# Hashed attention and a layer-norm feed-forward on one core: the row scale behind the second product, another start, loads and preparations at other places

## The chip, the cores and the metric

The kernel runs on one core of one Trainium2 chip. A core has five engines that run their own instruction streams in order: TensorE (PE in the profile, with its weight loads as PEld), VectorE (DVE), ScalarE (ACT), GpSimd (POOL) and SyncE (SP). They meet through semaphores. Data moves between the main memory and the on-chip memory through 16 DMA engines; SP, ACT and POOL issue the transfers. Products of PE land in PSUM, a small memory that DVE and ACT empty.

The metric is the device time of one execution in microseconds (us). Besides it there is one profiled execution, with a record of every instruction; its span is the time from the first instruction to the last.

## The reference: what is computed

Attention with 4 batches, 8 heads, 768 rows and 64 columns per head. Each row of q and of k gets a bucket number of six bits, and only rows of the same bucket attend to each other. The result, with its 8 heads side by side (512 columns), goes through a layer norm and a feed-forward with 2048 hidden units and a residual.

```python
q_bits = (np.einsum('bhsd,dk->bhsk', q, proj) > 0)      # proj: 64 x 6
mask = q_bucket[:, :, :, None] == k_bucket[:, :, None, :]
scores = np.where(mask, scale * q @ k^T, -1e9)
attn = softmax(scores) @ v                              # 4 x 8 x 768 x 64
x = attn, heads side by side                            # 4 x 768 x 512
xn = (x - mu) / np.sqrt(var + 1e-06) * g_ln
out = x + np.maximum(xn @ w_ch1, 0.0) @ w_ch2
```

## The kernel before

**Units, steps, batches.** A unit is four heads of one batch, so there are 8 units (n = 0 to 7), two per batch. A unit has 24 steps (4 heads x 6 row tiles), a batch has 48, and the whole main loop has 192. In step i, `scores` (L413) multiplies 128 rows of k with all 768 rows of q (two products of 384 columns, L420) and ACT takes the exponential (L426); `attend` (L429) works two steps behind, with six products per step (L437). After the last tile of a head DVE divides and writes 64 columns of x (L449, L454, L455).

**The mask inside the product.** The six hash bits of each row are written beside its 64 values as plus or minus one half (for q times 800), so that a product over 70 rows gives the score and the mask together. Preparing one unit's k, and likewise its q, takes: a cast to bf16 into one of three `pads` on POOL (L137 or L148), a 32x32 block transpose of the values on DVE (`hash_turn`, tile hashT, one buffer), the product with proj on PE (`hash_mm_wide` L159 for units 0 and 1, `hash_mm` L189 for the others), a transpose of the result on DVE into `bits` (L163 or L196) and the bits into the pad (L167, L172 or L199, L203), and a transpose of the pad into `opT`: on PE for units 0 and 1 (`turn_wide`, L212, emptied by DVE L219 and ACT L217), by a DMA transpose from SP for units 2 to 7 (`turn`, L224). For v, POOL casts and adds (L230 to L235), and PE sums over all rows (`value_sum`, L241).

**What sets the order.** Each engine's order is the order of the code. `at(i, fn, ...)` puts a piece of work into step i, and `plan_unit(n)` (L246) spreads the preparation of unit n over the 24 steps of unit n-1 and puts the loads of unit n+1 between them. All loads but the first q go through SP's queue, and a load that waits for a free buffer holds what stands behind it. Buffers that matter: `hashnat` (2), `scorenat` (3), `hashT` (1), `opT` (4), and two PSUM buffers "mm" that the hash products, the PE transposes, the value sums and both feed-forward products share.

**Weights.** The 8.4 MB of weights arrive in 16 pieces (L291), which borrow the space of `hbuf` and `x`, and DVE casts them to bf16 (L298 with the factor g_ln, L302).

**Layer norm and feed-forward.** Statistics of x are gathered along the way (`stat`, L311). After the last step of a batch `rstd` (L313) finishes the means and variances (L317, L319) and finds 1/sigma with four Newton rounds of four small DVE instructions (L332 to L338). `normalize` (L348) then writes (x - mean)/sigma in two halves, `turn_x` (L357) transposes each by DMA, and `feed_forward` (L369) runs seven steps after the batch's last step: 64 products of the first kind per half (L378), emptied by DVE (L387) and ACT (L385) in turn, then 48 of the second (L393), whose sums DVE adds to x (L399) before the store. The feed-forward of batch b is a generator of which some 4.7 products are issued per step of batch b+1; that of the last batch runs after the main loop.

## Time and profile before

| | us |
|---|---|
| three runs | 391.26, 392.71, 386.02 (median 391.26) |
| the profiled execution | 386.11, of it span 384.2 |
| first scores of unit 0 | 30.88 after the start |
| first scores of unit 2 (step 48) | 88.72 |
| first feed-forward product | 104.73 |
| last x of the last batch done, first product of its feed-forward | 323.27, 335.60 |

Over the span PE is busy 84 %, DVE 54 %, ACT 52 %, POOL 19 %. The shares hide stages with different limits, so the profile is read by stages: the start up to the first scores, the first batch, the three stretches around a layer norm inside the main loop, and the end. In a table of stages "PEclk" is the share of its full clock that PE was granted, and the DMA share is the mean busy share of the 16 DMA engines.

### The profile page before, as it was taken

Reading aid. Unit: us, or ns where it says so; the run is one execution under the profiler, and the core shown is the slowest. Engines: PE = TensorE matmul, PEld = TensorE weight load, DVE = VectorE, ACT = ScalarE, POOL = GpSimd, SP = SyncE. Lnnn points to the kernel's source line nnn. Section 1 sums busy time; section 2 is a strip of 40 time slices with the busy share of each in tenths; the row PEclk is TensorE's granted clock in tenths of the full one; section 3 lists DMA queues with packets and bytes.
Section 4 is the critical chain, followed back from the end, with each engine's and each line's share of the span. In section 5 each row is a group of like instructions: output and inputs, shape, how many; then the busy total and the mean of one; then the engine's idle time right before and its main releaser. Section 6 shows DMA issues by size and latency. Waiting matters only on the chain.

```text
span 384.2 us, 6912 instructions
## 1 busy us (share of the span) xinstructions
PE 323.8 (84%) x2741; PEld 187.5 (49%) x2760; DVE 205.6 (54%) x496; ACT 198.5 (52%) x261; POOL 72.1 (19%) x76
## 2 busy tenths in 40 slices
PE   0678988827289999995999999959999999599995
PEld 0344655514146555652565556525655665254542
DVE  0343779975944555568444555794433555642321
ACT  1015589944348656762587568625876783031220
POOL 8366011615011420420105012400000000000000
PEclk9966999975769999998999999998999999899999
DMA  8559999994399598703994999028401000510102
GB/s 165 159 165 373 285 287 355 203 234 132 83 224 220 145 243 239 167 27 84 253 252 127 211 235 214 22 43 184 83 2 51 33 2 3 122 42 30 55 0 82
DMA packets 77168, 56.03 MB, mean 146 GB/s; under 512 B 52560, under 2 KB 70992, under 8 KB 77136
## 3 DMA queue, kind: packets, MB, share of 16 engines
q1 hardware_dynamic: 76304, 54.80, 57.9%
q10 hardware_dynamic: 576, 0.79, 1.0%
q8 instruction: 21, 0.34, 0.4%
q14 instruction: 11, 0.09, 0.1%
q0 software_dynamic: 256, 0.01, 0.1%
HBM read 36.71 MB, written 6.29 MB: 112 GB/s over the span
## 4 chain that ended last, share of the span: by engine, by line
PE 58%; DVE 20%; DMA 15%; issue 2%; ACT 2%; SPq 1%; POOL 1%; DVEq 0%; ACTq 0%
PE sc L420 11%; PE av L437 6%; DMA hashnat<-in_k_dram 5%; DVE x L455 3%; DMA scorenat<-in_v_dram 3%; DMA hashnat<-in_q_dram 3%; DVE xn L348 2%; DVE nd L449 2%; DMA wst<-in_moe_w_ch_dram 2%; DMA opT<-pad_98 2%; DVE x L399 2%; PE hp L189 2%; ACT expb L426 2%; PE hpw L159 1%; PE o_4214 L393 1%
## 5 line engine op out<-in xcount | busy, mean ns | idle before, releaser
L426 ACT ACTIVATE expb<-sc,bias_sb 128x768 bf16<-128x768 f32 x192 | 168.4, 905 | 97.2 <-PE sc L420 95.7
L420 PE MATMUL sc<-opT 70*128 70x384 bf16 x384 | 97.9, 338 | 15.1 <-DMA opT<-pad_98 8.6
L437 PEld LDWEIGHTS <-expb 128*128 128x128 bf16 x1152 | 62.5, 99 | 28.0 <-issue 3.7
L378 PEld LDWEIGHTS <-w_sb 128*128 128x128 bf16 x512 | 45.1, 98 | 36.9 <-issue 15.4
L420 PEld LDWEIGHTS <-opT 70*128 70x128 bf16 x384 | 37.3, 100 | 49.0 <-issue 26.4
L393 PEld LDWEIGHTS <-hbuf 128*128 128x128 bf16 x384 | 34.6, 99 | 49.4 <-issue 19.3
L449 DVE TENSOR_TENSOR nd<-av,vd 128x390 f32<-128x390 f32 x32 | 17.9, 559 | 32.7 <-PE av L437 32.6
L178 DVE STREAM_TRANSPOSE hashT<-hashnat 128x768 f32<-128x768 f32 x32 | 29.2, 950 | 9.0 <-DMA hashnat<-in_k_dram 9.0
L159 PE MATMUL hpw<-hashT,projB 128*128 128x384 f32 x32 | 17.3, 706 | 11.6 <-DVE hashT L178 11.6
L437 PE MATMUL av<-vaug_103,expb 128*128 128x65 bf16 x432 | 25.5, 196 | 0.0
L437 PE MATMUL av<-vaug_102,expb 128*128 128x65 bf16 x432 | 25.5, 196 | 0.0
L455 DVE TENSOR_TENSOR x<-nd,rec 128x384 f32<-128x384 f32 x32 | 20.5, 641 | 1.1
L437 PE MATMUL av<-vaug_104,expb 128*128 128x65 bf16 x288 | 17.2, 197 | 0.0
L311 DVE BATCH_NORM_STATS2 stats<-x 128x6 f32<-128x256 f32 (+1 forms) x48 | 17.0, 381 | 0.3
L159 PEld LDWEIGHTS hpw<-hashT,projB 128*128 128x128 f32 x32 | 8.5, 278 | 17.6 <-DVE hashT L178 11.4
L217 ACT COPY opT<-tp 70x768 bf16<-70x768 bf16 x4 | 3.2, 795 | 23.7 <-PE tp L212 23.7
L233 POOL TENSOR_TENSOR scorenat<-scorenat 128x768 f32<-128x768 f32 x8 | 15.1, 1890 | 0.2
L137 POOL CAST pad_98<-scorenat 128x1536 bf16<-128x1536 f32 x4 | 5.9, 1467 | 46.1 <-DMA scorenat<-in_k_dram 25.1
L137 POOL CAST pad_96<-scorenat 128x1536 bf16<-128x1536 f32 x4 | 5.9, 1467 | 45.5 <-DMA scorenat<-in_k_dram 24.9
L137 POOL CAST pad_97<-scorenat 128x1536 bf16<-128x1536 f32 x4 | 5.9, 1467 | 40.7 <-DMA scorenat<-in_k_dram 21.0
L189 PE MATMUL hp<-hashT,projT 128*32 128x192 f32 x192 | 11.6, 365 | 1.4 <-DVE hbuf L387 1.4
L163 DVE STREAM_TRANSPOSE bitsw<-hpw 128x384 f32<-128x384 f32 x8 | 4.7, 583 | 14.6 <-PE hpw L159 14.6
(368 smaller groups left out, 430.1 us busy)
## 6 DMA issues: line engine op xcount, KB each, us to landing
wst<-in_moe_w_ch_dram SPq DMA_DIRECT2D x16, 512.0 KB, 9.5
hashnat<-in_k_dram SPq DMA_DIRECT2D x32, 192.0 KB, 4.4
scorenat<-in_v_dram SPq DMA_DIRECT2D x8, 768.0 KB, 5.1
out_dram<-x SPq DMA_DIRECT2D x24, 256.0 KB, 2.1
hashnat<-in_q_dram SPq DMA_DIRECT2D x28, 192.0 KB, 4.7
scorenat<-in_k_dram SPq DMA_DIRECT2D x6, 768.0 KB, 7.1
scorenat<-in_q_dram SPq DMA_DIRECT2D x6, 768.0 KB, 6.9
hashnat<-in_q_dram ACTq DMA_DIRECT2D x4, 192.0 KB, 6.2
```

The source lines that it names most:

```text
L137: nc.gpsimd.tensor_copy(pad_of(n, key)[:, :, 0:D], sn.rearrange("p h (s d) -> p (h s) d", d=D))
L159: nc.tensor.matmul(hp[:, 0 : w * 32], projB[:, j, :], hT[:, 2 * f : 2 * f + 2, :, j, :], start=(j == 0), stop=(j == 1),)
L178: nc.vector.transpose(hT[:, 2 * i : 2 * i + 2].rearrange("p c s j t -> p (c s j t)"), hn[:, 2 * i : 2 * i + 2].rearrange("p c n -> p (c n)"),)
L189: nc.tensor.matmul(hp[c * 32 : (c + 1) * 32, 0 : NS * 32], projT[:, j, :], hT[:, c, :, j, :], start=(j == 0), stop=(j == 1),)
L311: nc.vector.bn_stats(norm[b][:, s, part, :], xs[b][:, s, c0:c1])
L378: nc.tensor.matmul(hp[:, 0:QH], w1_sb[:, o, n * P : (n + 1) * P], xT[:, :, o, :], start=(o == 0), stop=(o == ND - 1),)
L393: nc.tensor.matmul(o2, hb[:, n, i * P : (i + 1) * P], w2_sb[:, n, :], start=(n == 0), stop=(n == NH - 1),)
L420: nc.tensor.matmul(sc[:, f, 0:QH], kT[0:KB, h * NS + t, :], qT[0:KB, h * NS + f * HALF : h * NS + (f + 1) * HALF, :],)
L426: nc.scalar.activation(e, sc[:, :, 0:QH], AF.Exp, scale=scale, bias=bias_sb)
L437: nc.tensor.matmul(av[:, s * VA : (s + 1) * VA], e[:, s // HALF, (s % HALF) * P : (s % HALF + 1) * P], va[:, h, t, :], start=(t == 0 and s ...
L449: nc.vector.tensor_add(nd, av[:, 0 : NS * VA].rearrange("p (s n) -> p s n", n=VA), vd[:, h : h + 1, :].to_broadcast([P, NS, VA]),)
L455: nc.vector.tensor_mul(xs[b][:, :, hd * D : (hd + 1) * D], nd[:, :, 0:D], rec.to_broadcast([P, NS, D]),)
```

## The change

What it does, part by part:

- **Row scale.** `normalize` only subtracts the mean. 1/sigma multiplies the sum of the second product instead (one `scalar_tensor_tensor` in place of the add, L394 of the changed kernel); since 1/sigma is positive it passes through the maximum with zero. `rstd` is split: `mean` stays ahead of `normalize`, and three Newton rounds (12 instructions and a factor, on POOL) follow four steps later.
- **Start.** proj is loaded once into `proj4` (4 small transfers in place of 8) and copied into projT and projB by 8 small DVE copies. 64 products of a constant tile (`WARM`) stand first on PE. The pieces of k and of q of unit 0 are spread over SP's and ACT's queues, k first on both. The casts and block transposes of k and q come before both hash products. The zeroing of the pads covers only the columns behind the bits and comes after the value work of unit 0.
- **Loads.** Unit 1's hash rows go into `scorenat` buffers and its v into a `hashnat` buffer; they and weight pieces 0 to 11 stand ahead of unit 2's loads in SP's queue, at the start of the program. Unit 2's loads stand at steps 3, 13 and 14, weight pieces 12 to 15 behind them. The casts of the weights stand 2 to 10 steps earlier.
- **Preparation.** Within a unit's plan, k is at +0, +2, +3 (cast and block transpose, hash product, transpose to opT), q at +4, +6, +7, v at +6 and +11; before they were at 0, 3, 5; 6, 9, 11; 9 and 15. For the odd units 3, 5 and 7 all of it is moved by 8 steps, so that it begins one step after the feed-forward of the batch before has taken up its place.

Three places in the order of the engines. On DVE around the first layer norm (names as above; `w_sb` are the cast weights, `pad_96` is unit 3's k), the kernel before has, at the end of the fourth Newton round:

```order
L334 TENSOR_TENSOR t<-t,ve 128x6
L335 TENSOR_SCALAR t<-t 128x6
L338 TENSOR_TENSOR y<-y,t 128x6
L348 TENSOR_SCALAR xn<-x,mv,y 128x512 x3
L302 CAST w_sb<-wst 128x1024
L348 TENSOR_SCALAR xn<-x,mv,y 128x512 x3
L196 STREAM_TRANSPOSE bits<-hp 128x192
L199 TENSOR_SCALAR pad_96<-bits 128x24x6
L302 CAST w_sb<-wst 128x1024 x3
L178 STREAM_TRANSPOSE hashT<-hashnat 128x768 x2
```

The changed kernel has at this place on DVE, with all of the layer norm in it:

```order
L291 CAST w_sb<-wst 128x1024
L306 BN_STATS stats<-x 128x6 x6
L308 BN_AGGR mv<-stats 128x2 x6
L342 TENSOR_SCALAR xn<-x,mv 128x512 x6
L318 TENSOR_SCALAR ve<-mv 128x6
L319 TENSOR_SCALAR t<-ve 128x6
L323 TENSOR_SCALAR y<-t 128x6
L448 TENSOR_TENSOR nd<-av,vd 128x390
L453 RECIPROCAL rec<-nd 128x6
L454 TENSOR_TENSOR x<-nd,rec 128x6x64
L172 STREAM_TRANSPOSE hashT<-hashnat 128x768 x2
L382 TENSOR_SCALAR hbuf<-h_1267 128x384
```

The Newton rounds, three weight casts and unit 3's hash bits are gone from between the statistics and the normalisation; one weight cast stands ahead of the statistics, and unit 3's first block transpose stands after the next head's division.

On DVE at the start of the program, the kernel before works through unit 0's k (`pad_96`) up to its last copy out of PSUM before q (`pad_97`) begins:

```order
L178 STREAM_TRANSPOSE hashT<-hashnat 128x768 x2
L163 STREAM_TRANSPOSE bitsw<-hpw 128x384 x2
L167 TENSOR_SCALAR pad_96<-bitsw 128x24x6
L219 COPY opT<-tp 70x24x32 x2
L178 STREAM_TRANSPOSE hashT<-hashnat 128x768 x2
L163 STREAM_TRANSPOSE bitsw<-hpw 128x384 x2
L167 TENSOR_SCALAR pad_97<-bitsw 128x24x6
L172 TENSOR_SCALAR pad_97<-pad_97 128x24x6
L219 COPY opT<-tp 70x24x32 x2
```

The changed kernel (k is `pad_93`, q is `pad_94`):

```order
L474 COPY projT<-proj_83 32x2x6
L475 COPY projB<-proj_83 32x2x6
L172 STREAM_TRANSPOSE hashT<-hashnat 128x768 x4
L157 STREAM_TRANSPOSE bitsw<-hpw 128x384 x2
L161 TENSOR_SCALAR pad_93<-bitsw 128x24x6
L157 STREAM_TRANSPOSE bitsw<-hpw 128x384 x2
L161 TENSOR_SCALAR pad_94<-bitsw 128x24x6
L166 TENSOR_SCALAR pad_94<-pad_94 128x24x6
L213 COPY opT<-tp 70x24x32 x4
```

The copies of proj now stand ahead of the block transposes, and q's block transposes ahead of k's bits; since hashT has one buffer, the third block transpose waits for k's hash product on PE.

On SP's queue the kernel before starts like this:

```order
L120 DMA hashnat<-in_k_dram 32x4x384 x8
L126 DMA scorenat<-in_v_dram 128x4x384
L120 DMA hashnat<-in_q_dram 32x4x384 x4
L126 DMA scorenat<-in_v_dram 128x4x384
L474 DMA g_sb<-in_moe_g_ln_dram 128x4x1
L291 DMA wst<-in_moe_w_ch_dram 128x1024 x8
L291 DMA wst<-in_moe_w_ch_dram 128x2x512
L120 DMA hashnat<-in_k_dram 32x4x384 x4
L126 DMA scorenat<-in_k_dram 128x4x384
L291 DMA wst<-in_moe_w_ch_dram 128x2x512 x3
L120 DMA hashnat<-in_q_dram 32x4x384 x4
L126 DMA scorenat<-in_q_dram 128x4x384
```

The changed kernel:

```order
L114 DMA hashnat<-in_k_dram 32x4x384 x2
L114 DMA hashnat<-in_q_dram 32x4x384 x2
L120 DMA scorenat<-in_v_dram 128x4x384
L114 DMA hashnat<-in_k_dram 32x4x384 x4
L114 DMA hashnat<-in_q_dram 32x4x384 x4
L466 DMA g_sb<-in_moe_g_ln_dram 128x4x1
L280 DMA wst<-in_moe_w_ch_dram 128x1024 x6
L120 DMA scorenat<-in_v_dram 128x4x384
L280 DMA wst<-in_moe_w_ch_dram 128x1024 x2
L280 DMA wst<-in_moe_w_ch_dram 128x2x512 x4
L114 DMA hashnat<-in_k_dram 32x4x384 x4
L120 DMA scorenat<-in_k_dram 128x4x384
```

Before, the second four of the k transfers, the four q transfers of unit 1 and unit 2's k each need a hashnat buffer back; in the changed kernel unit 1's rows take buffers that nothing has used, and all weight pieces up to the twelfth stand ahead of unit 2's first load.

The diff, cut to its core:

```diff
-    projT = consts.tile([P, 2, 32], F32)
...
+    proj4 = consts.tile([P, 2, NB], F32)
+    for h in range(UH):
+        nc.gpsimd.dma_start(
+            out=proj4[h * 32 : (h + 1) * 32], in_=proj.rearrange("(j p) n -> p j n", p=32)
+        )
...
-    for t in pads:
-        nc.gpsimd.memset(t[:, :, D:P], 0.0)
...
-        z = (n - 1) * UNIT
+        z = (n - 1) * UNIT + (8 if n % NU else 0) * (n > 1)
...
-        at(z + 0, cast, n, "k")
-        at(z + 0, hash_turn, n, "k")
-        at(z + 3, mm, n, "k")
...
+        for d, key in ((0, "k"), (4, "q")):
+            at(z + d, cast, n, key)
+            at(z + d, hash_turn, n, key)
+            at(z + d + 2, mm, n, key)
+            if wide(n):
+                at(z + d + 3, turn_wide, n, key, (nc.vector,))
+            else:
+                at(z + d + 3, turn, n, key)
+        at(z + 6, value_cast, n)
+        at(z + 11, value_sum, n)
+        if 2 < n + 1 < B * NU:
+            at(z + 2, load_hash, k, n + 1, "k", (nc.sync,))
+            at(z + 2, load_rows, k, n + 1, "k")
+            at(z + 6, load_hash, q, n + 1, "q", (nc.sync,))
+            at(z + 6, load_rows, q, n + 1, "q")
+            at(z + 9, load_rows, v, n + 1, "v")
...
-    def rstd(b):
+    def mean(b):
         stats = norm[b]
...
+    def rstd(b):
+        mv = norm[b]
...
-        for _ in range(4):
-            nc.vector.tensor_mul(t, y, y)
...
+        nc.gpsimd.tensor_scalar_mul(ve, ve, -0.5)
+        for _ in range(3):
+            nc.gpsimd.tensor_mul(t, y, y)
+            nc.gpsimd.tensor_mul(t, t, ve)
+            nc.gpsimd.tensor_scalar_add(t, t, 1.5)
+            nc.gpsimd.tensor_mul(y, y, t)
+        rstds[b] = y
...
-                xn[:, i, :], xs[b][:, s, :], scalar1=mv[:, s, 0:1],
-                scalar2=y[:, s : s + 1], op0=AOP.subtract, op1=AOP.mult,
+                xn[:, i, :], xs[b][:, s, :], scalar1=mv[:, s, 0:1], scalar2=None,
+                op0=AOP.subtract,
...
-                nc.vector.tensor_add(x[:, s, :], o2, x[:, s, :])
+                nc.vector.scalar_tensor_tensor(
+                    x[:, s, :], o2, rstds[b][:, s : s + 1], x[:, s, :],
+                    op0=AOP.mult, op1=AOP.add,
+                )
...
-    load_hash(k, 0, "k", nc.sync)
-    load_hash(q, 0, "q", nc.scalar)
+    both = (nc.sync, nc.scalar)
+    load_hash(k, 0, "k", both)
+    load_hash(q, 0, "q", both)
+    load_rows(v, 0, "v")
+    load_hash(k, 1, "k", (nc.sync,), "scorenat", 3)
+    load_hash(q, 1, "q", (nc.sync,), "scorenat", 3)
+    nc.sync.dma_start(out=g_sb, in_=moe_g_ln.rearrange("(o p) -> p o", p=P))
+    load_weights("hbuf", 2, (0, 1, 2))
+    load_weights("hbuf", 2, (3, 4, 5))
+    wp = ps_mm.tile([P, 512], F32, tag="mm", name="wp")
+    for _ in range(WARM):
+        nc.tensor.matmul(wp[:, 0:P], delta_m, delta_m)
+    for h in range(UH):
+        r = slice(h * 32, (h + 1) * 32)
+        nc.vector.tensor_copy(projT[r, :, h * NB : (h + 1) * NB], proj4[r])
+        nc.vector.tensor_copy(projB[r, :, h * 32 : h * 32 + NB], proj4[r])
     for key in ("k", "q"):
         cast_wide(0, key)
         hash_turn(0, key)
...
+    load_rows(v, 1, "v", "hashnat", 2)
+    load_weights("x", 3, (6, 7, 8))
+    load_weights("x", 3, (9, 10, 11))
+    hash_mm_wide(0, "k")
+    hash_mm_wide(0, "q")
+    turn_wide(0, "k", (nc.vector, nc.scalar))
+    turn_wide(0, "q", (nc.vector, nc.scalar))
     value_cast(0)
...
+    for t in pads:
+        nc.gpsimd.memset(t[:, :, KB:P], 0.0)
...
-        at(z + BATCH, rstd, b)
+        at(z + BATCH, mean, b)
         at(z + BATCH, normalize, b, 0)
         at(z + BATCH + 1, turn_x, b, 0)
         at(z + BATCH + 1, normalize, b, 1)
-        at(z + BATCH + 3, turn_x, b, 1)
+        at(z + BATCH + 2, turn_x, b, 1)
+        at(z + BATCH + 4, rstd, b)
```

89 lines of the change are left out of this document (26 added, 63 removed).

## The prediction, made before the changed kernel was run

> **What bounds the kernel now.** I read the stages first, then who waited for whom, then the chain that ended last. In the table of stages the columns after the window are its length, the busy time of PE, PEld, DVE, ACT and POOL with instruction counts, the granted clock, the DMA share and GB/s:
>
> ```profile
> 10.00:31.00 21.00, 15.10 (x66) 8.45 (x67) 9.29 (x17) 3.18 (x4) 11.67 (x14) 0.81 0.61 173
> 31.00:53.00 22.00, 19.74 (x174) 12.86 (x173) 13.01 (x25) 12.21 (x15) 5.53 (x6) 0.87 1.05 342
> 53.00:80.00 27.00, 22.85 (x298) 15.07 (x295) 24.95 (x44) 25.86 (x33) 8.07 (x7) 1.00 1.11 257
> 80.00:89.00 9.00, 0.45 (x8) 0.18 (x5) 3.85 (x9) 1.03 (x2) 1.47 (x1) 0.56 1.11 259
> 171.00:185.00 14.00, 9.77 (x73) 4.84 (x73) 10.36 (x43) 4.30 (x5) 0.00 (x0) 0.88 0.48 106
> 250.00:264.00 14.00, 9.76 (x78) 4.97 (x78) 9.99 (x40) 3.88 (x5) 0.00 (x0) 0.88 0.52 96
> ```
>
> In the first 31 us little runs beside a chain of preparations, and the DMA engines are only 0.61 busy. From 31 to 89 they are full (over 1 by the profile's count). From 80 to 89 no engine does anything. At two layer norms inside the main loop (171, 250) PE is busy 9.8 us of 14 at 0.88 of its clock. Who waited (engine, line, for whom: total, times, longest):
>
> ```profile
> PE sc L420 <- DMA opT<-pad_98: 8.6, 1, 8.6
> PE h_1225 L378 <- DMA xT<-xn: 6.5, 1, 6.5
> PE o_2218 L393 <- DVE bits L196: 4.2, 1, 4.2
> PE o_4214 L393 <- DVE x L399: 4.2, 1, 4.2
> ```
>
> These waits are single and long: unit 2's q transpose, the first normalised x, a hash result standing behind the layer norm on DVE, and a sum standing behind it there. And the chain that ended last, from 25 us on:
>
> ```profile
> 25.13 8.65 DMA wst<-in_moe_w_ch_dram
> 33.86 10.92 DMA hashnat<-in_k_dram
> ...
> 57.47 10.99 DMA scorenat<-in_v_dram
> ...
> 80.32 8.26 DMA opT<-pad_98
> ```
>
> So transfers pace the first batch: the end of the first 89 us is set by the order in which SP's queue feeds the DMA engines.
>
> **1. The start.** The chain of waits begins with the block transposes and goes through two hash products (8 records each):
>
> ```profile
> 1.32 2.27 POOL L71 DMA_DIRECT2D projT<-in_proj_dram  x4 [0.88 <-DVE bias_sb L83]
> DMA to landing us min/median/max: 5.7/7.0/7.5
> 10.36 1.84 DVE L178 STREAM_TRANSPOSE hashT<-hashnat 128x768 f32<-128x768 f32 x2 [9.00 <-DMA hashnat<-in_k_dram]
> 11.44 5.17 PE L159 MATMUL hpw<-hashT,projB 128*128 128x384 f32 x8 [11.44 <-DVE hashT L178]
> 20.98 5.46 PE L159 MATMUL hpw<-hashT,projB 128*128 128x384 f32 x8 [0.18 <-DVE hashT L178]
> 30.88 1.44 PE L420 MATMUL sc<-opT 70*128 70x384 bf16 x4 [0.42 <-ACT opT L217]
> 44.33 2.83 PE L159 MATMUL hpw<-hashT,projB 128*128 128x384 f32 x8
> ```
>
> From the first block transpose to the first scores it is 20.5 us (30.88 - 10.36). The changed kernel's DVE must first copy proj. Its four transfers no longer wait for DVE, so I let them issue from 0.45 on, 0.57 each (2.27/4); the last, at 2.1, lands 5.7 to 7.5 later, at 7.8 to 9.6. With two copies of about 0.2 the block transposes start at 8.2 to 10.0; I take 8.7, since k now comes first in both queues and even the last of the eight pieces of k and q was there at 10.36.
>
> From there the chain depends on PE's speed. A product pair takes 2.83 us at 44 us and 5.2 to 5.5 at the start. Walking through the new order (two 0.92 us block transposes, k's products, q's block transposes, which need hashT back, bits, q's products, 8 groups of transposes through two PSUM buffers) with the old durations, I get 15.5 us to the first scores with fast products and 20.4 with slow ones. So side by side alone gives nothing; all hangs on the warmed PE. The 64 small products start at about 1 us, when their constant tile is written. A slow one should take 0.12 us (128 columns, where a record of 384 took 0.36 in the slow first scores, 1.44/4), a fast one half of that, so they end between 5 (all fast) and 9 (all slow). The first hash product needs one block transpose first, at 9.8: an idle stretch of 1 to 5 us. What a gap does to the clock (window, length, PE busy, clock, DMA share, GB/s):
>
> ```profile
> 28.00:29.00 1.00, 0.69 (x14) 1.00 0.63 176
> 29.00:30.00 1.00, 0.92 (x12) 0.93 0.51 162
> 30.00:31.00 1.00, 0.52 (x3) 0.50 0.90 340
> ```
>
> PE was busy 0.69 and 0.92 of two of these and yet fell to half its clock at 30. So a gap need not be wholly idle to cost the clock, and I expect it to fall somewhere before or in the first pair and come back within it or the second. I take the middle, 18 us: first scores at 26.7 (between 23.7 = 8.2 + 15.5 and 30.4 = 10.0 + 20.4), 4.2 us earlier.
>
> The Trainium skill (TensorE: Matmul & The Clock Gate, section "What's actually happening") states that a free-running window of about 3.4 us decides, and that the clock halves after an idle window. By that most gaps of this length would keep the clock and the first scores would come at 24.2; the rows above, a fall after two mostly busy microseconds, do not agree with "idle" taken literally, and the measurement decides.
>
> **2. Steps 0 to 47.** Unit 1's preparation is packed into steps 0 to 7. PE runs in order, and with only one step between hash product and transpose it waits about 0.4 us each time for the bits, with fewer exponentials beside; I put 1.1 us (0 to 2). In the run before unit 2's first block transpose came 28.3 us after the first scores:
>
> ```profile
> 59.20 1.83 DVE L178 STREAM_TRANSPOSE hashT<-hashnat 128x768 f32<-128x768 f32 x2
> 65.37 11.17 SPq L224 DMA_TRANSPOSE opT<-pad_97  x1
> 76.63 3.09 SPq L120 DMA_DIRECT2D hashnat<-in_q_dram  x4
> 80.32 6.17 SPq L224 DMA_TRANSPOSE opT<-pad_98  x1
> 109.60 5.13 SPq L224 DMA_TRANSPOSE opT<-pad_96  x1
> ```
>
> Now: 26.7 + 28.3 + 1.1 = 56.1. Unit 2's k transpose was issued 6.2 later and held SP for 11.17 us behind a backlog of weights; the next k transpose held it 5.13. The new queue has no hole between 10 and 31 us, where 39 % of the DMA time went unused (8 us), so the weights should be through by about 57. Then: k transpose two steps (1.6 us) nearer, issued at 60.7; SP free at 66; from the q loads to the q transpose landed it was 12.0 us (76.63 to 80.32 + 8.26); q landed at 78. PE without a wait would reach step 48 at 56.1 + 20.9 = 77 (before: 88.72 less the wait of 8.6, less 59.20). First scores of unit 2 at 78.3 instead of 88.72: **-10.4** (this holds the 4.2 and the 1.1). If the backlog stays whole it is 5.6 us later, -4.8; at best, with the earliest start, -14.8.
>
> **3. The first layer norm.**
>
> ```profile
> 94.84 0.17 DVE L323 TENSOR_SCALAR ve<-mv 128x6 f32<-128x6 f32 x1
> 99.52 1.46 DVE L348 TENSOR_SCALAR xn<-x,mv,y 128x512 bf16<-128x512 f32 x3
> 24.09 0.72 POOL L234 TENSOR_TENSOR scorenat<-scorenat 128x256 f32<-128x256 f32 x1
> 88.00:96.00 8.00, 6.93 (x65) 0.58 0.33 102
> 104.00:113.00 9.00, 6.88 (x47) 0.57 1.10 216
> ```
>
> The Newton rounds took 4.7 us between the mean and xn; one weight cast of 0.7 now stands ahead instead: **-4.0**, out of a wait of 6.5, so about 2.5 of that wait stays. PE ran at 0.58 and 0.57 of its clock in the stretches after the two waits, some 3 us lost in each; with short waits I take back 2.5 of it (0 to 5.9): **-2.5**. The 13 instructions on POOL cost at most 13 x 0.72 = 9.4 us. They hide behind the 80 feed-forward products ahead of the first sum, 17 steps; uncovered they would cost those 9 us per batch. The multiply-add takes the add's place on the same 512 columns; I cost it at nothing (hidden except at the end, where one stands in the open).
>
> **4. Layer norms two and three.** No hash bits and no Newton rounds stand in DVE's way there now, only 4.4 us of means and subtractions, and the sum under way has a second PSUM buffer free. From the stage rows: 14 - 9.77 = 4.2 idle and 0.12 x 14 = 1.7 of clock, 5.9 each: **-11.8** (at least the two idle times, -8.4).
>
> **5. The last one.**
>
> ```profile
> 324.77 0.17 DVE L323 TENSOR_SCALAR ve<-mv 128x6 f32<-128x6 f32 x1
> 328.61 1.46 DVE L348 TENSOR_SCALAR xn<-x,mv,y 128x512 bf16<-128x512 f32 x3
> 335.60 0.81 PE L378 MATMUL h_4235<-xT,w_sb 128*128 128x384 bf16 x4
> ```
>
> x was ready for the subtraction at 324.77 and waited to 328.61; the first product follows 7.0 us after that in any case (subtraction and transpose): **-3.8**.
>
> **6. What it costs.** In units 3, 5 and 7 q's transpose moves from step +11 to +15 of 24, so its cover shrinks from 13 steps to 9, of 1.6 us each. In the run before, unit 3's:
>
> ```profile
> 117.36 8.46 SPq L224 DMA_TRANSPOSE opT<-pad_97  x1
> DMA to landing us min/median/max: 7.1/9.2/11.2
> 130.81 0.49 PE L420 MATMUL sc<-opT 70*128 70x384 bf16 x2
> ```
>
> It was issued at 117.36 and took the longer of the two times to landing that the trace gives for this stretch, 11.2 us, so it was there at 128.6; the unit's first scores came at 130.81. After the change k's transpose is issued some 5 us after the feed-forward begins, and if q lands 19 us after that, as before (109.6 to 128.6), the same 2 us are left. Also the hash products follow their block transposes after two steps, not three. Together **+3** (0 to 8).
>
> **The sum.** -10.4 - 4.0 - 2.5 - 11.8 - 3.8 + 3 = -29.5. From the profiled execution's 386.11 that is 356.6. The profile lies at the low end of the runs (386.02 to 392.71, median 391.26); for a median I add half of that distance, 2.5: **359**.
>
> **Rivals.**
> - *The clock holds.* If PE keeps its clock through the gap, both pairs take 2.8 us and the first scores come 2.5 earlier than my middle: 356.5. Against it the fall at 30 us. The Trainium skill (the page and section named above) would have it so. 0.12.
> - *The warming does nothing.* The clock falls before k's products and both pairs take over 5 us, as before: 2.4 later, 361.5, and the start is worth 1 to 2 us. 0.17.
> - *The transfers stay late.* Between 10 and 89 us 20 MB were moved (the GB/s of the four first rows times their lengths). If the DMA engines' pace and not the holes sets the end of that, unit 2's q lands at 84 to 86 whatever starts earlier, and 5.6 to 8 us of part 2 are gone: 366. For it the full DMA share from 31 to 89; against it the 8 us unused before 31. 0.14.
> - *Slower: transposes of the odd units come late.* Place: steps 72, 120 and 168, where PE stands, in order, before scores whose opT is still in flight. Beyond the margin of 2 us, a lateness of L costs 3 x L, of which the 3 of part 6 hold L = 1. L from 3 to 13 gives 365 to 395; from 14.4 on, with q landing 27 us after its issue where this one took 11.2, it is slower than before by 2 %. 0.12: 0.03 below 383, 0.05 up to 399, 0.04 slower.
> - *The forecast*, 0.45.
>
> About 2 % is what a measurement of this kernel can tell from no change, given how its runs scatter. Range: 349 to 373. Below, the best start with every other term at its best would give 386.1 - 14.8 - 4.0 - 5.9 - 11.8 - 3.8 = 346, and they will hardly all come together; above stand the late transfers with the full friction, 366 + 5, and a little for the scatter. The late transposes of the last rival mostly lie outside. Faster: 0.45 + 0.12 + 0.17 + 0.14 + 0.03 = 0.91; same 0.05; slower 0.04.
>
> **What would show it.** Right: first scores near 27 us; records of 0.35 us in at least one of the first two hash pairs; first scores of unit 2 near 78 after a wait under 2 us; no PE wait of 4 us at the two inner layer norms, and a granted clock near 1 there; 8.5 us from the last x to its feed-forward's first product, not 12.3 (335.60 - 323.27). Wrong: SP held over 10 us by unit 2's k transpose; PE waiting for opT at steps 72, 120 or 168; DVE waiting for POOL's 1/sigma; long waits for bits in steps 0 to 8.

## The result, and the profile after

The changed kernel takes **366.56 us** in the median of four runs (363.37 to 369.49), the kernel before 390.94 beside it (386.02 to 392.71). The ratio is 0.9389 with a 95 % interval of 0.9247 to 0.953: faster by some 6 %, and 7.6 us slower than the 359 forecast. (The ratio is taken without 369.49 and 392.71, slow runs over 1.5 % above the fastest of their kernel.) The profiled execution took 367.68 us (span 365.9), where the sum had 356.6. So 11.1 us of the predicted gain are missing.

The stages of the changed kernel, with the columns of the table in the prediction (window, length, busy time of PE, PEld, DVE, ACT and POOL, granted clock, DMA share, GB/s):

```profile
10.00:32.00 22.00, 13.60 (x65) 7.93 (x66) 11.91 (x23) 3.18 (x4) 14.82 (x14) 0.77 1.07 331
...
70.00:87.00 17.00, 17.00 (x141) 10.86 (x138) 10.27 (x26) 14.40 (x16) 0.00 (x0) 0.50 1.17 243
165.00:179.00 14.00, 13.01 (x121) 7.31 (x121) 9.42 (x27) 7.58 (x9) 8.95 (x18) 1.00 0.56 133
238.50:252.50 14.00, 11.76 (x104) 6.65 (x107) 9.62 (x25) 7.19 (x9) 8.97 (x18) 0.94 0.50 95
```

Two things are as forecast: the DMA engines now work from 10 us on (a share of 1.07, before 0.61), and PE is busy 13.0 and 11.8 us of 14 at the two inner layer norms (before 9.8). Two are not: the first stretch ends no earlier than before, and from 70 to 87 us PE has no idle time by its records and still runs at half its clock. Who waited for whom:

```profile
PE hpw L153 <- DVE hashT L172: 6.2, 1, 6.2
...
PE h_1267 L373 <- DMA xT<-xn: 1.7, 1, 1.7
```

The long waits of before (8.6, 6.5 and three of 4.2; the list in the prediction leaves out the one of `o_3282` for the hash bits, at the second of the inner layer norms) are gone or down to 1.7. What leads the list now is at the start. Its records (columns: start, busy time, engine, line, operation; in brackets the idle time before it and what ended it):

```profile
1.08 5.67 PE L471 MATMUL wp<-delta_m 128*128 128x128 bf16 x64 [1.08 <-DVE delta_m L70]
...
1.31 2.38 POOL L77 DMA_DIRECT2D proj_83<-in_proj_dram  x4 [0.88 <-POOLq L564]
...
10.11 1.47 POOL L142 CAST pad_94<-hashnat 128x1536 bf16<-128x1536 f32 x1 [2.15 <-DMA hashnat<-in_q_dram]
...
10.24 1.36 DVE L474 COPY projT<-proj_83 32x12 f32<-32x12 f32 x1
...
11.96 1.84 DVE L172 STREAM_TRANSPOSE hashT<-hashnat 128x768 f32<-128x768 f32 x2
...
13.00 5.49 PE L153 MATMUL hpw<-hashT,projB 128*128 128x384 f32 x8 [6.25 <-DVE hashT L172]
...
20.88 4.21 PE L153 MATMUL hpw<-hashT,projB 128*128 128x384 f32 x8 [2.40 <-DVE bitsw L157]
...
32.01 0.81 PE L419 MATMUL sc<-opT 70*128 70x384 bf16 x4 [0.77 <-ACT opT L211]
```

The warming ends at 6.75 (1.08 + 5.67), the first hash product stands at 13.00: a hole of 6.25 us in front of the pair that was to be warm, and it takes 5.49, as slow as before. The first scores come at 32.01 (before 30.88). And the chain that led to unit 2's first scores (step 48), in SP's queue and on DVE:

```profile
61.87 1.82 DVE L172 STREAM_TRANSPOSE hashT<-hashnat 128x768 f32<-128x768 f32 x2
...
66.40 6.42 SPq L218 DMA_TRANSPOSE opT<-pad_94  x1
...
76.49 6.36 SPq L218 DMA_TRANSPOSE opT<-pad_95  x1
...
87.05 0.83 PE L419 MATMUL sc<-opT 70*128 70x384 bf16 x2
...
97.65 1.44 PE L373 MATMUL h_1267<-xT,w_sb 128*128 128x384 bf16 x4 [1.68 <-DMA xT<-xn]
```

The inner batches from mean to mean (the second batch's mean to the third's, the third's to the fourth's), and from the fourth mean to the end. The kernel before:

```profile
171.82:250.40 78.58, 72.80 (x670) 42.74 (x675) 45.59 (x117) 49.29 (x64) 15.64 (x14) 0.98 0.73 172
250.40:324.05 73.65, 68.23 (x622) 40.39 (x626) 37.08 (x104) 46.31 (x61) 0.00 (x0) 0.98 0.23 51
324.05:384.20 60.15, 51.45 (x249) 24.58 (x250) 21.68 (x57) 7.86 (x16) 0.00 (x0) 0.97 0.18 53
```

The changed kernel:

```profile
165.08:238.55 73.47, 71.08 (x669) 42.25 (x675) 44.32 (x100) 49.29 (x64) 18.57 (x27) 1.00 0.81 183
238.55:311.19 72.64, 68.13 (x622) 40.45 (x626) 36.98 (x89) 46.18 (x61) 10.58 (x20) 0.98 0.26 52
311.19:365.90 54.71, 50.04 (x249) 24.32 (x250) 18.86 (x41) 7.84 (x16) 2.71 (x13) 1.00 0.19 58
```

Of the 18.3 us by which the span is shorter (384.2 - 365.9), 16.1 lie behind the first mean, which stood at 94.12 and stands at 91.89 (290.1 against 274.0), 2.2 ahead of it. From the second mean to the third PE is now busy 71.1 us of 73.5 at full clock; there is next to nothing left to take there but PE's own work. Ahead of the first mean, where the forecast had its largest single term, almost nothing was won.

### The profile page after: what moved, and what is told of

Its sections match the earlier page's. It is cut to its first block, busy times and chain, and to the rows that moved or that the text cites. A ratio compares the mean times of both kernels' runs of the same rounds, so it can differ in the third digit from the quotient of the medians.

```text
span 365.9 us, 7023 instructions
## 1 busy us (share of the span) xinstructions
PE 329.3 (90%) x2803; PEld 195.4 (53%) x2824; DVE 200.3 (55%) x440; ACT 200.2 (55%) x261; POOL 81.4 (22%) x124
## 4 chain that ended last, share of the span: by engine, by line
PE 71%; DVE 17%; DMA 5%; issue 3%; ACT 2%; SPq 0%; DVEq 0%; ACTq 0%
PE sc L419 15%; PE av L436 8%; PE hpw L153 4%; DVE x L454 3%; PE hp L183 2%; DVE nd L448 2%; DMA scorenat<-in_v_dram 2%; DVE w_sb L287 2%; DVE x L394 2%; DVE hashT L172 2%; PE tp L206 1%; ACT expb L425 1%; DMA out_dram<-x 1%; DMA xT<-xn 1%; DMA hashnat<-in_k_dram 1%
## 5 line engine op out<-in xcount | busy, mean ns | idle before, releaser
L425 ACT ACTIVATE expb<-sc,bias_sb 128x768 bf16<-128x768 f32 x192 | 170.2, 903 | 83.0 <-PE sc L419 79.8
L419 PE MATMUL sc<-opT 70*128 70x384 bf16 x384 | 103.4, 353 | 4.9 <-ACT expb L425 1.7
L436 PEld LDWEIGHTS <-expb 128*128 128x128 bf16 x1152 | 66.4, 103 | 31.5 <-issue 9.4
L448 DVE TENSOR_TENSOR nd<-av,vd 128x390 f32<-128x390 f32 x32 | 17.9, 561 | 28.3 <-PE av L436 28.2
L436 PE MATMUL av<-vaug_97,expb 128*128 128x65 bf16 x432 | 28.6, 208 | 0.0
L436 PE MATMUL av<-vaug_96,expb 128*128 128x65 bf16 x432 | 25.1, 194 | 0.0
L454 DVE TENSOR_TENSOR x<-nd,rec 128x384 f32<-128x384 f32 x32 | 23.5, 733 | 1.1
L153 PE MATMUL hpw<-hashT,projB 128*128 128x384 f32 x32 | 15.3, 637 | 8.6 <-DVE hashT L172 6.2
L436 PE MATMUL av<-vaug_98,expb 128*128 128x65 bf16 x288 | 18.1, 202 | 0.0
L153 PEld LDWEIGHTS hpw<-hashT,projB 128*128 128x128 f32 x32 | 7.3, 238 | 14.6 <-DVE hashT L172 6.4
L190 DVE STREAM_TRANSPOSE bits<-hp 128x192 f32<-128x192 f32 x12 | 4.5, 377 | 13.2 <-PE hp L183 13.0
L131 POOL CAST pad_94<-scorenat 128x1536 bf16<-128x1536 f32 x4 | 6.3, 1568 | 21.7 <-DMA scorenat<-in_k_dram 13.4
L342 DVE TENSOR_SCALAR xn<-x,mv 128x512 bf16<-128x512 f32 x24 | 9.7, 471 | 0.0
```

The source lines that it names most:

```text
L153: nc.tensor.matmul(hp[:, 0 : w * 32], projB[:, j, :], hT[:, 2 * f : 2 * f + 2, :, j, :], start=(j == 0), stop=(j == 1),)
L419: nc.tensor.matmul(sc[:, f, 0:QH], kT[0:KB, h * NS + t, :], qT[0:KB, h * NS + f * HALF : h * NS + (f + 1) * HALF, :],)
L425: nc.scalar.activation(e, sc[:, :, 0:QH], AF.Exp, scale=scale, bias=bias_sb)
L436: nc.tensor.matmul(av[:, s * VA : (s + 1) * VA], e[:, s // HALF, (s % HALF) * P : (s % HALF + 1) * P], va[:, h, t, :], start=(t == 0 and s ...
L448: nc.vector.tensor_add(nd, av[:, 0 : NS * VA].rearrange("p (s n) -> p s n", n=VA), vd[:, h : h + 1, :].to_broadcast([P, NS, VA]),)
L454: nc.vector.tensor_mul(xs[b][:, :, hd * D : (hd + 1) * D], nd[:, :, 0:D], rec.to_broadcast([P, NS, D]),)
```

## The experiments

The questions were three. Which part of the change carries the gain? Why did the start bring nothing? And what is the long stretch at half clock, and what does it cost? Each comparison with a single run has the scatter of such runs in it (the changed kernel's four lie 6 us apart), so the arguments go by stages of the traces.

### The scale alone, and everything but the scale

The kernel before with only the scale part (`normalize` subtracts only, three Newton rounds on POOL follow, and the add behind the second product becomes the multiply-add):

```diff
-        at(z + BATCH, rstd, b)
+        at(z + BATCH, mean, b)
         at(z + BATCH, normalize, b, 0)
...
+        at(z + BATCH + 4, rstd, b)
```

> The kernel before with the scale part alone: x - mean goes to the transpose at once, 1/sigma is finished on POOL and multiplied in the add behind the second product. If the Newton rounds were what the layer norms cost, the wait for the first xT falls from 6.5 to about 2.5 us, the two waits of 4.2 us in the loop shrink to under 1, and the last x to its first product takes 8.5 us and not 12.3: about 4 + 8 to 12 + 4 = 16 to 20 us less than before, 370 to 374. The rival: the two waits in the loop come from the hash products of the next unit that stand inside the layer norm on DVE, and stay without the shift of 8 steps; then only the first and the last layer norm gain, 8 us, 382.

The changed kernel with four Newton rounds back on DVE ahead of the subtraction, which multiplies again, and the plain add:

```diff
-        at(z + BATCH, mean, b)
+        at(z + BATCH, rstd, b)
         at(z + BATCH, normalize, b, 0)
...
-        at(z + BATCH + 4, rstd, b)
```

> The changed kernel with the Newton rounds back on DVE ahead of the subtraction, and the plain add; everything else as changed. If the scale part carries the gain at the layer norms, this is 16 to 20 us slower than the changed kernel: 382 to 387, with waits of about 4 us at both inner layer norms. If the shift of the odd units' preparation by 8 steps is what freed the inner ones, they stay free of waits over 2 us and only the first and the last layer norm lose, about 4 + 4 us: 374.

Measured: the scale alone 368.41 against 387.94 of the kernel before beside it, 19.5 less; all but the scale 382.83, 5.1 less. The two add up to 24.6, and the whole change gave 24.4 (390.94 - 366.56); with single runs an agreement that close is partly chance. So about four fifths of the gain are the row scale's. The traces say the same: from the first mean to the end it is 270.6 us with the scale alone (366.60 - 96.01), 274.0 in the changed kernel and 290.1 before. The same stretches with the scale alone:

```profile
169.79:243.16 73.37, 70.81 (x670) 42.19 (x675) 44.46 (x101) 49.24 (x64) 18.66 (x27) 1.00 0.81 184
243.16:311.86 68.70, 66.36 (x622) 39.79 (x626) 35.96 (x88) 46.26 (x61) 9.18 (x19) 1.00 0.24 55
311.86:366.60 54.74, 50.03 (x249) 24.30 (x250) 18.85 (x41) 7.85 (x16) 2.70 (x13) 0.99 0.20 58
```

And all but the scale:

```profile
171.57:248.35 76.78, 71.11 (x669) 42.27 (x675) 47.28 (x116) 49.29 (x64) 15.81 (x14) 1.00 0.80 175
319.82:381.00 61.18, 52.43 (x249) 24.93 (x250) 21.67 (x57) 7.84 (x16) 0.00 (x0) 0.93 0.17 52
```

With the scale alone each inner batch is about 5 us shorter than before (78.58 to 73.37, 73.65 to 68.70), the end 5.4, and from the first mean to the first feed-forward product it is 5.7 us instead of 10.6 (96.01 to 101.71; before 94.12 to 104.73; with all but the scale it stays at 10.0). With everything else but the scale the inner batches are some 2 us shorter (76.78, and 71.47 for the next), the end not at all. The rival, that the hash products standing inside the layer norm made the 4.2 us waits, falls as the main cause of the time: with them in their old place and the Newton rounds gone, the batches are as short as in the whole change or shorter. As a cause of those waits it stands beside the Newton rounds: PE waits 1.2 us at most between the second mean and the fourth with the scale alone, and 1.7 at most with all but the scale. So the 4.2 us took both, and either part of the change ends them; but only the scale takes 5 us out of a batch. From the third mean to the fourth it is shorter with the scale alone (68.70) than in the whole change (72.64, of which 1.7 are a fall of the clock at 250 us); so in these traces the packed and shifted preparation gives some of it back there.

### The start

Without the 64 warming products:

```diff
-    wp = ps_mm.tile([P, 512], F32, tag="mm", name="wp")
-    for _ in range(WARM):
-        nc.tensor.matmul(wp[:, 0:P], delta_m, delta_m)
```

> The 64 warming products are left out, nothing else. Theory A (the warmed clock is lost in the 6.25 us between the last warming product and the first hash product): k's pair stays at 5.2 to 5.5 us, q's at 4.2 to 5.5, first scores within 32.0 +1.3/-0.3 us. Theory B (the warming is what made q's pair 4.2 us instead of 5.5, and so keeps part of the clock): q's pair 5.5, first scores at 33.3. If the stretch at half clock from 70 to 101 us comes from the order of this kernel, it shows again at about the same step (24 to 30); if it is a chance of the one profiled run, it is gone or elsewhere.

With 176 of them:

```diff
-    WARM = 64
+    WARM = 176
```

> 176 warming products in place of 64, so that they last to about 13 us (112 more at 0.056). Theory A: the clock holds, the first hash pair takes 2.8 us in place of 5.5, q's pair 2.8 to 4.2; first scores 2.7 to 4.9 us earlier, 27.1 to 29.3. If the chain is bound by DVE or the transfers at that point, first scores stay at 32.0 +-0.5.

With proj's four transfers on SP and ACT, ahead of k and q, instead of POOL:

```diff
     for h in range(UH):
-        nc.gpsimd.dma_start(
+        (nc.sync, nc.scalar)[h % 2].dma_start(
             out=proj4[h * 32 : (h + 1) * 32], in_=proj.rearrange("(j p) n -> p j n", p=32)
```

> The four small proj transfers are issued from SP and ACT ahead of k and q, not from POOL. Theory A (the start is late because proj lands at 10 us and its copies then stand behind POOL's cast): block transposes start at 6.5 to 7.5 instead of 11.96, the gap after the warming products is under 2 us, the first hash pair runs at full clock (2.8 to 3.5 us) and the first scores come at 22 to 27 (22 if both pairs are fast: 6.6 + 15.5; 27 if both are slow: 6.6 + 20.4). Rival (small pieces of 24 bytes are slow on any queue): proj lands after 9 us, first scores at 30 or later.

Measured, with one run each: 367.53 without warming, 361.11 with the long one, 360.62 with the early proj (before: 389.79; the late casts below were run beside these). Without warming:

```profile
13.19 4.89 PE L153 MATMUL hpw<-hashT,projB 128*128 128x384 f32 x8 [13.19 <-DVE hashT L172]
...
31.93 0.81 PE L419 MATMUL sc<-opT 70*128 70x384 bf16 x4 [0.77 <-ACT opT L211]
```

The 64 products are worth nothing in the changed kernel: slow pairs (4.89 and 4.54) and the same first scores without them (31.93, 32.01). With 176 of them, which end at 12.42:

```profile
12.38 1.84 DVE L172 STREAM_TRANSPOSE hashT<-hashnat 128x768 f32<-128x768 f32 x2
...
13.42 2.85 PE L153 MATMUL hpw<-hashT,projB 128*128 128x384 f32 x8 [1.00 <-DVE hashT L172]
...
28.75 0.81 PE L419 MATMUL sc<-opT 70*128 70x384 bf16 x4 [0.77 <-ACT opT L211]
```

Both pairs take 2.85 us (the second from 18.66), and from the block transpose it is 16.4 us to the first scores (28.75 - 12.38), where the prediction had worked out 15.5 for fast products. So the warming does what it was meant to, if it ends close enough to the first product (1.00 us ahead of it here). With proj early:

```profile
2.58 0.16 DVE L474 COPY projT<-proj 32x12 f32<-32x12 f32 x1 [1.22 <-DMA proj<-in_proj_dram]
...
7.75 1.84 DVE L172 STREAM_TRANSPOSE hashT<-hashnat 128x768 f32<-128x768 f32 x2 [4.17 <-DMA hashnat<-in_k_dram]
...
8.78 2.85 PE L153 MATMUL hpw<-hashT,projB 128*128 128x384 f32 x8 [2.62 <-DVE hashT L172]
...
28.18 1.44 PE L419 MATMUL sc<-opT 70*128 70x384 bf16 x4 [0.66 <-ACT opT L211]
```

proj is there at 2.6 us, the block transposes wait for k alone, the hole before k's pair is 2.62 and the pair fast; but the clock falls at 14.16, after the wait of 2.39 between the pairs, and q's pair is slow (4.54). First scores at 28.18. The long warming had the same wait of 2.39 and kept its clock. The clock's changes lie multiples of some 3.4 us apart (more on this below), and here one such stretch held the whole wait (window, length, PE busy and so on, as above):

```profile
10.75:14.16 3.41, 1.02 (x4) 0.33 (x3) 2.49 (x4) 0.00 (x0) 2.09 (x2) 1.00 1.11 289
```

There it lay across two, with PE busy 2.10 and 2.33 us of 3.41 (14.17 to 17.58, 17.58 to 20.99). So that both pairs were fast with 176 products is in part luck of where the wait fell; a wait of that length can cost the clock or not.

All of it together: proj early, 110 warming products, 46 more between the pairs, and the three POOL memsets of the pads (1.26 us each) moved behind the first scores.

```diff
+    wf = ps_av.tile([P, 512], F32, tag="av", name="wf")
+    for _ in range(46):
+        nc.tensor.matmul(wf[:, 0:P], delta_m, delta_m)
     hash_mm_wide(0, "q")
...
-    WARM = 64
+    WARM = 110
```

> The changed kernel with the start put together from what the earlier runs showed: proj's four small transfers on SP and ACT ahead of k and q, 110 warming products instead of 64, so that PE is busy up to the first block transpose's end at about 8.7 us, 46 more between the two hash pairs (2.4 us, the wait seen there), and the three memsets on POOL moved behind the first scores. Theory, that the start's missing gain is the late proj and the two holes of PE: both pairs take 2.85 us, the first scores come at 8.7 + 15.5 = 24 us and not 32, unit 2's first block transpose at 54, and the whole is about 8 us under the changed kernel: 357 to 359. The rival, that the transfers of unit 2 end this stretch whatever starts earlier: first scores at 24, but unit 2's first scores not before 83, and 362 to 364.

```profile
9.69 2.80 PE L153 MATMUL hpw<-hashT,projB 128*128 128x384 f32 x8
...
25.63 0.81 PE L419 MATMUL sc<-opT 70*128 70x384 bf16 x4 [0.77 <-ACT opT L211]
...
54.39 1.83 DVE L172 STREAM_TRANSPOSE hashT<-hashnat 128x768 f32<-128x768 f32 x2
...
61.14 10.40 SPq L218 DMA_TRANSPOSE opT<-pad  x1
...
83.56 0.80 PE L419 MATMUL sc<-opT 70*128 70x384 bf16 x2 [0.35 <-DMA opT<-pad]
```

Both pairs are fast (the second 2.84), the first scores come at 25.63, even ahead of the 26.7 of the prediction, and unit 2's block transpose at 54.39, 7.5 earlier than in the changed kernel. But unit 2's k transpose now holds SP for 10.40 us where it was 6.42, its q transpose goes out at 74.95 (76.49 in the changed kernel), and unit 2's first scores come at 83.56. The k transpose was issued at 61.14, 64.00, 64.32 and 66.40 (all together, long warming, proj early, changed), 5.3 us apart; SP was free of it at 71.54, 70.20, 69.93 and 72.82, only 2.9 apart and not in that order. That is as the rival has it. Of 6.4 us at the start 3.5 are left at step 48 (87.05 - 83.56). In four runs the kernel takes 365.31 (361.72 to 367.08), a ratio of 0.9418 to the kernel before (0.9347 to 0.9489): no difference from the changed kernel's 0.9389 that could be told. The rival, that unit 2's transfers end this stretch whatever starts earlier, had 83 us and 362 to 364; it came closer than the theory.

Step 48 over these runs: first scores at 32.01, 31.93, 28.75, 28.18, 25.63 (changed, no warming, long warming, proj early, all together) gave unit 2's first scores at 87.05, 86.29, 82.11, 82.10, 83.56. A start 3 to 4 us better comes through in full; what lies beyond that did not, in the one trace that has it. The two single runs at 361 lie 2 to 3 us under the fastest run of the changed kernel; the kernel with all edits together, in four runs, did not show more than its scatter. Part of that scatter goes with the clock: the changed kernel's runs of 363.37, 365.45, 367.68 and 369.49 us were granted 0.962, 0.956, 0.939 and 0.941 of it over the span, the two at 361 0.976. So some of their 2 to 3 us may be where the clock happened to fall.

### The long stretch at half clock

The clock fell at 70 us in the changed kernel, after a stretch in which PE waited for DVE (block transposes behind two weight casts):

```profile
66.60:70.00 3.40, 1.90 (x29) 0.99 (x25) 3.40 (x7) 1.79 (x3) 0.00 (x0) 1.00 1.05 254
```

PE was busy 1.90 of 3.40 us, and from 70.00 to 100.7 us the clock stood at half. The first trial takes the casts out of DVE's way (pieces 6 to 11 ten steps later, 12 to 15 four):

```diff
-        at(26 + w, cast_weights, w + 6)
+        at(36 + w, cast_weights, w + 6)
     for w in range(12, 16):
-        at(34 + w, cast_weights, w)
+        at(38 + w, cast_weights, w)
```

> The casts of weight pieces 6 to 11 and 12 to 15 go back to steps 36 to 41 and 50 to 53, as in the kernel before; all else as changed. Theory A (the clock fell at 70 us because PE waited, in one window, for a block transpose that stood on DVE behind these casts): PE's wait of 1.4 us before unit 2's q hash product is gone, the clock stays at 1.00 through steps 28 to 48, steps of 0.79 us, first scores of unit 2 some 4 to 5.5 us earlier relative to step 24 (20.9 to 22 us after unit 2's first block transpose, not 26.1). Theory C (the casts are not the cause, or the fall is a matter of chance): the clock falls again between steps 24 and 34.

```profile
70.00:82.00 12.00, 10.06 (x122) 6.62 (x121) 10.38 (x26) 12.00 (x16) 0.00 (x0) 1.00 1.18 214
82.00:86.00 4.00, 0.56 (x8) 0.32 (x6) 0.52 (x2) 1.42 (x2) 0.00 (x0) 0.80 1.20 268
```

No fall at 70, and PE reaches step 48 earlier; there it stands for 3.8 us until unit 2's q has landed (first scores at 86.36, 87.05 in the changed kernel), and the clock falls then, to 0.50 until 105 us. The time is the same: 365.89. So the 8.5 us of PE's work that the half clock takes away between 70 and 87 us cost the kernel less than 1 us at step 48, because the transfers would have ended that stretch anyway. The slow PE hid the wait. What the half clock costs from there to 101 us this run does not show, since it has it too.

Then, what brings the clock back? In the changed kernel it did not return through the attention products, the first 17 us of them without a gap (70 to 87 in the table of stages), and came back 3.1 us after the first feed-forward product (97.65). To test whether full products do it, 16 of them (128 rows, 512 columns) were put in at step 40, and as a control 21 of the scores' form (70 rows, 384 columns):

```diff
+    def burst():
+        bt = ps_mm.tile([P, 512], F32, tag="mm", name="burst")
+        for _ in range(16):
+            nc.tensor.matmul(bt[:, 0:512], ident, w1_sb[:, 0, 0:512])
+
+    at(40, burst)
```

> The changed kernel with 16 full products (128 rows, 512 columns, some 3.4 to 6.8 us of PE) put in at step 40, inside the stretch of 31 us that ran at half clock with PE busy by all its records. Theory: attention products alone (70 rows, 65 columns) do not bring the clock back and dense ones do, so a clock of 1.00 returns within about 7 us of the burst, some 15 us earlier than in the changed kernel, and the steps after it take 0.79 and not 0.97 us. The rival: the clock's return has nothing to do with what PE computes, and it stays at 0.50 until the feed-forward at about 100 us. If the clock does not fall near 70 us this time, neither is tested.

> The control: 21 products of the scores' form (70 rows, 384 columns; as many columns in all) at the same step 40. By the theory of dense products the clock stays at 0.50 after this one up to the feed-forward; if any uninterrupted row of products brings it back, it returns here as after the dense burst; if neither does, the burst is no cause.

Neither was a test: the clock did not fall near 70 this time (it stayed at 1.00 to 98 us in both; 368.16 and 364.04). The clock's changes in a trace lie multiples of about 3.4 us apart (in the changed kernel it is low from 11.98 to 18.81 and from 70.00 to 100.71, 2 and 9 times 3.41), as if by windows that run on their own, and these lie elsewhere in each run; I take it that here none held enough of the wait. It also means that the late casts of the run before need not be what kept the clock at 70 us: these two runs kept it with the casts in their place. The pair was run again with a wait for POOL's memsets at step 32, meant to make the fall certain:

```diff
+    def hole():
+        for _ in range(32):
+            nc.gpsimd.memset(hole_sb, 0.0)
+        bt = ps_mm.tile([P, 512], F32, tag="mm", name="hole")
+        nc.tensor.matmul(bt[:, 0:P], hole_sb[:, 0:P], delta_m)
...
+    at(32, hole)
     at(40, burst)
```

> The changed kernel with a hole made on purpose: at step 32 PE waits for 32 small memsets on POOL, about 6 us, so that the clock must fall near 75 us; and at step 40 the 16 full products of 128 rows and 512 columns follow (6.8 us at half clock). Theory of dense products: the clock is back at 1.00 within some 7 us of the burst's start, before the first feed-forward product, and stays. The rival, that what PE computes plays no part: after the hole the attention products, busy by all records, bring the clock back by themselves within 4 to 8 us, before the burst; or nothing brings it back until the feed-forward.

> The same hole, followed at step 40 by 21 products of the scores' form (70 rows, 384 columns), the same number of columns in a row without a wait. Theory of dense products: the clock stays at 0.50 through the burst and on to the first full products of the feed-forward, some 25 to 30 us in all, as in the changed kernel. The rival, that any unbroken row of products does it: the clock returns at the burst as in the run with dense ones.

PE did not have to wait for the memsets, so they made no hole (the product behind them ran at 73 us); but the clock fell at 69 in both, after three microseconds in which PE was busy 1.44 and 1.67. With full products, which stand from 81.23 on:

```profile
81.20:83.00 1.80, 1.80 (x10) 0.70 (x8) 0.00 (x0) 0.89 (x1) 0.00 (x0) 0.50 1.09 346
83.00:98.00 15.00, 13.07 (x141) 8.16 (x140) 10.00 (x34) 11.84 (x16) 0.00 (x0) 1.00 0.37 99
```

With the scores' form, from 80.98 to 87.9:

```profile
81.00:88.00 7.00, 7.00 (x26) 3.31 (x24) 0.00 (x0) 0.83 (x1) 0.00 (x0) 0.50 0.98 272
88.00:105.00 17.00, 15.41 (x128) 10.06 (x127) 12.92 (x42) 14.42 (x16) 1.80 (x8) 0.50 0.17 33
```

Two microseconds of full products brought the clock back at 83 us. Seven microseconds of 70-row products without a gap did not, and it stayed at half for 41 us, up to 5 us after the first feed-forward product (105.10). The rival, that any unbroken row of products does it, falls in this pair, one trace each. It agrees with the other traces: in all ten where the clock fell between 64 and 86 us (the kernel before, the changed one and eight of the variants) it came back 2 to 9 us after the next wide products over all 128 rows, be they the feed-forward's, the hash's or the burst, and never ahead of them. (The attention's own 128-row products are 65 columns wide. A single one of 260 columns, the value sum, fell into six of these stretches and ended none, nor did hash products that were under way when the clock fell.) What it is worth in time the pair shows only roughly: 370.47 and 372.97, one run each.

The Trainium skill (TensorE: Matmul & The Clock Gate, section "What's actually happening") states that the clock is full after one busy window of some 3.4 us. The traces do not agree with that for these products: 17 us without a gap in the changed kernel, and 7 in the run with the 70-row burst, did not release it. Whether the rows, the columns or the share of both in the array decide was not separated.

### The last trial

The start put together, and in addition: three of the last four weight pieces (1.6 MB) behind unit 2's q transpose, casts 6 to 11 at steps 14 to 22, the first six casts two steps earlier, and 12 full products at step 44 as a filler in the wait. Cut to the loads and the filler:

```diff
-    at(15, load_weights, "hbuf", 2, (12, 13, 14))
-    at(18, load_weights, "hbuf", 2, (15,))
+    at(15, load_weights, "hbuf", 2, (15,))
+    at(32, load_weights, "x", 3, (12, 13, 14))
...
+    at(44, fill)
```

> The run with the start put together, with two more edits. Three of the last four weight pieces (1.6 MB) are loaded behind unit 2's q transpose and not ahead of its k transpose, and pieces 6 to 11 are cast at steps 14 to 22, ahead of unit 2's block transposes on DVE; and 12 full products (2.6 us) stand at step 44, where PE would wait for the q transpose. Theory, that after the earlier start the transfers ahead of unit 2's q transpose set the end of this stretch: the k transpose holds SP for 5 to 6 us and not 10.4, unit 2's first scores come at 78 to 79 and not 83, no stretch of half clock of over 10 us follows, and the whole takes about 355. The rival, that the casts and products merely move the waits: unit 2's first scores stay at 82 or later and the time at 361 to 365.

```profile
58.41 1.82 DVE L172 STREAM_TRANSPOSE hashT<-hashnat 128x768 f32<-128x768 f32 x2
...
63.77 5.99 SPq L218 DMA_TRANSPOSE opT<-pad  x1
...
82.18 0.48 PE L419 MATMUL sc<-opT 70*128 70x384 bf16 x2
```

The k transpose holds SP for 5.99 and not 10.40 us, the number of the theory (the filler took 2.75 us at 77.27), and no long stretch at half clock follows (0.985 over the span). That the moved weights did it is not shown: this transpose was issued 2.6 us later, at 63.77, and those issued at 64.00 and 64.32 with the weights in their old place (long warming, proj early) held SP for 6.20 and 5.61. But the earlier casts push unit 2's block transpose on DVE from 54.39 to 58.41, and step 48 comes at 82.18: the rival's number. 363.88 us (360.5 to 371.71), ratio 0.9358 (0.9258 to 0.9458): again not to be told from the changed kernel, though two of the four runs (360.5 and 361.37) lie under its fastest. Whether weights and casts can be laid so that both come early stays open.

## Why the prediction was right, and where it was not

It said faster, 359 us within 349 to 373, and it is 366.56. It was right by its terms for the layer norms, which gave 16.6 of the 19.1 us forecast; of the largest term, the 10.4 us up to step 48, only 1.7 came, and the range was wide enough to hold that. The account by its own parts, on the profiled execution:

| part | predicted | measured |
|---|---|---|
| 1 and 2, up to unit 2's first scores | -10.4 | -1.7 (88.72 to 87.05) |
| 3, from there to the first feed-forward product | -6.5 | -5.4 (16.0 to 10.6) |
| 4, 5 and 6, from there to the end | -12.6 | -11.2 (279.5 to 268.25) |
| sum | -29.5 | -18.3 |

**Part 1 failed, and it is the step that failed first.** The sentence was "I let them issue from 0.45 on ... With two copies of about 0.2 the block transposes start at 8.2 to 10.0; I take 8.7". The four transfers of proj issued from 1.31 on, and there were eight copies and not two, the last six from 9.99 to 11.93, one at 1.36 us instead of 0.16 beside a cast on POOL that began at 10.11. So the block transposes stood at 11.96, 3.3 late. That made the hole before k's pair 6.25 us where the prediction had 1 to 5, and both pairs slow: 20.1 us to the first scores (32.01 - 11.96), near the slow end of 20.4, and not the middle of 18. Together 5.3 us. "All hangs on the warmed PE" was right, as the runs with 176 products and with everything together showed (25.63); the warming that the change has does nothing behind a proj that comes this late.

**Part 2: the chain was right, its start and its slack were not.** From the first scores to unit 2's block transpose it took 29.9 us (predicted 28.3 + 1.1), from there to its k transpose's issue 4.5 (4.6), and that held SP for 6.42 (5.13). The records of unit 2's q transpose alone give its time to landing:

```profile
DMA to landing us min/median/max: 8.5/8.5/8.5
```

76.49 + 8.5 = 85.0, where the prediction had 78: 5.8 of the 7 us from the block transpose (61.87, not 56.1), 1.2 from SP. The other 2.1 us to 87.05 are PE at half clock. This is what the rival *The transfers stay late* put at 84 to 86 us and 366 in all, with a chance of 0.14, and it is what was measured; in the changed kernel itself by luck, since 5.8 of those 7 us are the late start and not the transfers' pace. Its mechanism, that this pace sets the end whatever starts earlier, is half shown: a start 3.3 to 3.8 us earlier came through in full, one 6.4 us earlier gave 3.5. The backlog that part 2 feared came back there, with a hold of 10.40 us, 5.3 over the 5.13 of the sum. (Its "5.6 us later" is not the difference of the two holds it shows, 11.17 - 5.13 = 6.0.)

**Part 3 held.** The wait for xT fell from 6.5 to 1.7. Newton's 4.7 us went: 10.6 us from the mean to the product became 5.8. The 2.5 of clock did not come: it stood at 0.50 through all of that stretch.

**Part 4: the mechanism held, its size was off.** From the stage rows, 4.2 us idle became 1.0 and 2.2, and the clock lost 0 and 0.8 us where it had lost 1.7: 7.7 of 11.8. The reason named the Newton rounds and the hash bits that stood in DVE's way. Either gone ends the 4.2 us waits, as the two runs with one part each show; but taking the first away was worth some 5 us a batch, and all else without it some 2.

**Part 5 was too small.** From the last statistics to the first product:

```profile
310.42 0.86 DVE L306 BATCH_NORM_STATS2 stats<-x 128x6 f32<-128x64 f32 x6
...
311.80 1.21 DVE L342 TENSOR_SCALAR xn<-x,mv 128x512 bf16<-128x512 f32 x3
...
317.17 0.81 PE L373 MATMUL h_4293<-xT,w_sb 128*128 128x384 bf16 x4
```

6.75 us where it was 12.33: 5.6 won, not 3.8. "The first product follows 7.0 us after that in any case" was wrong: it now follows 5.4 us after the subtraction begins (317.17 - 311.80), since the subtraction without the factor is shorter (1.21 for 1.46) and the transpose went through faster (issued at 313.04, 4.1 us ahead of the product; before 5.5).

**Part 6.** What is left over of parts 4 to 6 is 2.1 us (7.7 + 5.6 - 11.2), where 3 stood. The slower rival, late transposes at steps 72, 120 and 168, did not come; PE waited for no opT there. POOL's Newton rounds hid as expected: no wait of DVE for them appears, and its instructions take 0.20 to 0.26 us each in the mean, not the 0.72 of the bound.

The multiply-add cost 0.74 us where the add cost 0.69. The rival *The warming does nothing* came true as well, but it had the first scores at 29 and counted the start as a gain of 1 to 2 us; it was a loss of 1.1. One reading of the prediction is too strong: from 80 to 89 us its own row shows DVE busy 3.85 us and ACT 1.03, so it was PE that did next to nothing (0.45), and not every engine.

## What to carry to other kernels

A factor per row that can pass behind a product should go there: what stood between a mean and a transpose on a serial chain was worth 19.5 us of 388 (one run), four fifths of the whole change, and it needed no rearrangement around it. A warming row is worth something only if it ends shortly before the first real product begins: 6.25 us ahead it was worth nothing, 2.62 and 1.00 us ahead that product was fast. So it is sized by the latest input (here proj, four pieces of 1.5 KB), not by a round number. And before a stretch of slow PE is fought, look at what would end it otherwise: here the transfers did, and keeping the clock up until that wait (365.89) or starting 6 us earlier (365.31) hardly moved the time.
